# Double output tiles stored 256 tokens at a time, with the orders and engines drawn anew, in a fused sparse attention and max-out kernel

## The chip, the cores and the metric

The kernel runs on one NeuronCore of a Trainium2 chip. The metric is the device time of one execution in microseconds (us). Each core has five engines that run side by side and meet through semaphores: TensorE (PE in the profile, with its weight loads as PEld), VectorE (DVE), ScalarE (ACT), GpSimd (POOL) and SyncE (SP), which here only issues transfers (DMAs).

## The reference

Inputs are q, k, v of shape (4 batches, 8 heads, 768 positions, 64) and three weights: w1 and w2 (512 x 1024) and w_out (1024 x 512), all float32.

```
k_sum = k.reshape(B, H, nb, 32, D).max(axis=3)       # one key per block of 32
v_sum = v.reshape(B, H, nb, 32, D).mean(axis=3)
scores_l = scale * q @ k^T, kept where |i - j| < 16
scores_s = scale * q @ k_sum^T + log(32)
a = softmax over [scores_l, scores_s]
x = a @ [v, v_sum]                                    # heads side by side: 3072 tokens x 512
out = maximum(x @ w1, x @ w2) @ w_out                 # 3072 x 512, float32
```

## The kernel before, in words

Work is cut by batch (b, 0 to 3), by pair of heads (hp, 0 to 3) and by group of 256 tokens (grp, 0 to 2, NG = 3). For every batch and pair, k, q and v are loaded (`load_kq` L450, `load_v` L461) into one of 13 landing tiles, cast to bf16 (`prep` L572, `cast_v` L471), and k and q are turned so that the head dimension lies on partitions: by PE (L593), or, for the pairs in `turn` (batch 2, pairs 2 and 3, and batch 3), by a transposing DMA (L597). The turned k is placed, its block maxima are taken (L619), and tails and maxima are put beside it. `scores` (L661) fills two PSUM banks per group, `weigh` takes the exponential on ACT (L675) and the mask on DVE (L685), `values` multiplies by v on PE (L717), DVE divides (L738, L741), and the result xs is turned into xt, by PE in batch 0 and by a DMA on SP (L747) in batches 1 to 3.

`maxout` (L821) uses max(h1, h2) = h1 + max(h2 - h1, 0). Weights wd = w2 - w1 are made on the chip (L777), and w1o = w1 @ w_out (`make_w1o`, L805, matmuls L813), which needs w1 turned (L787) and w_out cast (L802). For each of the 12 groups there are four "hidden" tasks (L829, 8 matmuls each), each followed by a relu on ACT (L838) or DVE (L840) into g, and two output tiles of 128 tokens (u = 0, 1). An output tile is three tasks on PE in one PSUM bank: x @ w1o (L856, 4 matmuls) and two halves of g @ w_out (L863, 4 matmuls each). Then ACT or DVE copies the bank into an SBUF tile `o` (L866), and SP stores that tile of 128 x 512 float32 (256 KB) in one DMA (L874). Tokens are shifted by 16, so the last tile of a batch wraps and takes two DMAs (L874 and L876). The very last tile is cut in three parts (256, 128 and 128 columns).

Nothing of the order is in program order. Each step is a task of a `Plan` (L116), with a priority from `CFG["prios"]` and, where there is a choice, an engine from `CFG["engines"]`, one entry a task. `Plan.run` (L182) plays the tasks through with durations written in the program and writes each engine's instructions in the order that comes out; what a queue then waits for, the whole queue behind it waits for. Buffers come from rings (`Ring`, L69): a task may take a slot only when the planner believes the slot's last user to be done. `osr` (L332) is the ring of output tiles, 4 slots. At most eight of SP's DMAs are under way: each waits for the eighth before it. Matmuls with no use (`filler`, L300) stand where the planner expects PE to be idle early.

Of the kernel before, what the change touches and what calls it, by code (L numbers as in the profile page):

```python
# [14 lines left out]
F32 = mybir.dt.float32  # L15
# [12 lines left out]
    turn="22 23 30 31 32 33", lx="SSS", cols=True,  # L28
)
CFG["prios"] = list(map(int, """  # L30
# [25 lines left out]
""".split()))  # L56
CFG["engines"] = "".join("""
PDDDPPADDDPPPPPPDPSSSDDDATDASSSDDPPTAASSSPPDPTAASSSPDPPTDDSSDPTASSPDTASSPATDSSDATASPSPSASPDTDTADPDADDTATADPPADATATDD
PPAAATPTDDAAPDTATDDTDTATDDTATATDDTDTATDDTDTATDDTATATDDTASSSDSSSASSSASSSPPDDPDDDATDDDDDATATADPDAADTATDDPADATADTDDSTAD
TDDSTADTDDSPTDTDDPAPDDTPTADDDPDTADTDDSTADTDDSTADTDDSSSSDSSSASSSASSSADPADPAAATAAPAPATATDDAAPDDTATADPPDDTADTDDSTADTDDS  # L60
TADTDDSDSASADPAPASDSDDPADTADTDDSTADTDDSTADTDDSSSSASSSASSSPSSSDPAPADSPDTDPPDAPSDSDDADDPSDSADDAATADTDDSTADTDDSTADTDDSA
SPSDDPPAASDSDDADATADTDDSTADTDDSTADTDDSTTATTDTTATTATDTDTATATTTASTTTASTATATATDTTTASTTTDSTATATATATTTASTTTDSTDTATDTDTTTA
STTTASTDTATDTDTTTASTTTASTATDTDTDTTTASTTTASTDTATDTDTTTASTTTDSTATATATATTTDSTTTASTDTATATDTTTASTTTASTATATDTDTTTDSTTTDSTA
TATDTATTTDSTTTASTDTATATATTTDSTTTASTTTDATTTDS
""".split())
ENG = {"T": "PE", "D": "DVE", "A": "ACT", "P": "POOL", "S": "SP"}

# [192 lines left out]
def kernel(  # L260
# [14 lines left out]
    nc = tc.nc  # L275
# [53 lines left out]
    xsr = Ring(tiles("xs", 4, [128, 2, 2, 2, D], BF16))  # L329
    xtr = Ring(tiles("xt", 6, [128, KC, GT], BF16))  # L330
    gr = Ring(tiles("g", 3, [128, FC, GT], BF16))
    osr = Ring(tiles("o", 4, [128, d_model], F32))  # L332
    wd = [Buf(Ring([t])) for t in tiles("wd", 4, [128, KC, 256], BF16)]
    w1br = Ring(tiles("w1b", 2, [128, KC, 256], BF16))
    w1b = [Buf(w1br) for _ in range(4)]
# [485 lines left out]
    def maxout(b, grp, prio):  # L821
        x, g = xt[b, grp], Buf(gr)
        for n in range(4):
            ps = Buf(banks, "mm")

            def hid(n=n, ps=ps):
                for s in range(2):
                    for c in range(KC):
                        nc.tensor.matmul(out=bank(ps)[:, 256 * s:256 * s + 256],  # L829
                                         lhsT=wd[n].ap[:, c, 128 * s:128 * s + 128],  # L830
                                         rhs=x.ap[:, c, :], start=(c == 0), stop=(c == KC - 1))

            op("T", 0.87, lambda e, hid=hid: hid(), words=16, read=[x, wd[n]], write=[ps], prio=prio, label=f"hidden {b}{grp}{n}")

            def relu(e, n=n, ps=ps):
                o = g.ap[:, 2 * n:2 * n + 2, :].rearrange("p f n -> p (f n)")
                if e == "A":
                    nc.scalar.activation(out=o, in_=bank(ps), func=ACT.Relu)  # L838
                else:
                    nc.vector.tensor_scalar_max(out=o, in0=bank(ps), scalar1=0.0)  # L840

            op("A", {"A": 0.6, "D": 0.69}, relu, read=[ps], write=[g], prio=-1, label=f"relu {b}{grp}{n}")
        last = b == B - 1 and grp == NG - 1
        for u in (1, 0) if last else (0, 1):
            o = Buf(osr)
            cuts = (0, 256, 384, 512) if last and u == 0 else (0, 512)
            for i, (c0, c1) in enumerate(zip(cuts, cuts[1:])):
                out_part(b, grp, u, x, g, o, c0, c1, prio, "D" if i == 1 else "A", i == 1)

    def out_part(b, grp, u, x, g, o, c0, c1, prio, engine, on_act):  # L850
        ps, cols, part = Buf(banks, "mm"), slice(c0, c1), (c1 - c0) / 512
        sl, done = slice(128 * u, 128 * u + 128), Buf(Ring([None]))

        def first():
            for c in range(KC):
                nc.tensor.matmul(out=bank(ps, c1 - c0), lhsT=x.ap[:, c, sl], rhs=w1o[c].ap[:, cols],  # L856
                                 start=(c == 0), stop=False)

        op("T", 0.87 * part, lambda e: first(), words=8, read=[x, *w1o], write=[ps], prio=prio + 1, label=f"out {b}{grp}{u}")
        for n in range(2):  # L860
            def more(n=n):
                for f in range(4 * n, 4 * n + 4):
                    nc.tensor.matmul(out=bank(ps, c1 - c0), lhsT=g.ap[:, f, sl],  # L863
                                     rhs=wo[f // 2].ap[:, f % 2, cols], start=False, stop=(f == FC - 1))
            op("T", 0.87 * part, lambda e, more=more: more(), words=8, read=[g, *wo], change=[ps], prio=prio + 1, label=f"out {b}{grp}{u}")
        copy(engine, {"A": 0.18 + 0.42 * part, "D": 0.15 + 0.55 * part}, lambda: (  # L866
            o.ap[:, cols], bank(ps, c1 - c0)),
             read=[ps], write=[o, done], prio=-1, port=False, label=f"copy out {b}{grp}{u}")

        def store(e):  # L870
            at = grp * GT + u * 128 + 16
            n = min(128, S - at)
            queue = nc.scalar if on_act else nc.sync
            queue.dma_start(out=out[b * S + at:b * S + at + n, cols], in_=o.ap[0:n, cols])  # L874
            if n < 128:
                queue.dma_start(out=out[b * S:b * S + 128 - n, cols], in_=o.ap[n:128, cols])  # L876

        op("A" if on_act else "S", 0.75 * part, store, read=[done], touch=[o], prio=-1, issue=0.65, label=f"store {b}{grp}{u}")

    def attention(b, base):  # L880
        for half in range(2):
# [78 lines left out]
```

## Time and profile before

| | us |
|---|---|
| median of 3 runs (lowest, highest) | 170.51 (169.4, 171.54) |
| the profiled execution | 169.97 |
| its span, from first to last recorded instruction | 168.2 |
| PE busy in it | 159.7 |

The profiled execution lies 0.54 us below the median, and 1.77 us of it lie outside the span. A group row of the profile names a line, an engine, the operation, the output and input tiles, the count, the busy time, the mean duration in ns, and the idle time before it with what ended it. The chain of waits is read from the end back: each piece is what released the next one. A DMA on SP has two times: how long SP was held by it (SPq), and how long after its issue the data had landed. The granted TensorE clock was 1.00 in every stage.

### The profile page before, as it was taken

How to read it: one execution, taken by the hardware profiler on the slowest of the kernel's cores; microseconds unless marked ns; L12 is line 12 of the kernel's file. 1: busy time of each engine (PE TensorE's matmuls, PEld its weight loads, DVE VectorE, ACT ScalarE, POOL GpSimd, SP SyncE). 2: the span in 40 equal slices, each digit the busy share in tenths (PEclk: the TensorE clock that was granted, in tenths of full speed). 3: DMA queues.
4: the chain of work that ended last, by engine and by line, in shares of the span. 5: the costliest groups of instructions: out<-in, count | busy, mean ns of one | idle time of the engine just before them, and what ended most of it. 6: DMA issues, size and time to landing. Idle time of an engine off the chain costs nothing.

```text
span 168.2 us, 4640 instructions
## 1 busy us (share of the span) xinstructions
PE 159.7 (95%) x1918; PEld 105.6 (63%) x1918; DVE 104.0 (62%) x207; ACT 104.5 (62%) x148; POOL 43.1 (26%) x73
## 2 busy tenths in 40 slices
PE   6999999989999999999999999979997999999992
PEld 4768757765676555667577555737564558568462
DVE  4778688663397898787695573849913867023031
ACT  4576888783697998887993578953365652024111
POOL 7506575056534000356330203330300000000000
PEclk9999999999999999999999999999999999999999
DMA  5999999999999999999888998989889336211033
GB/s 166 337 227 329 283 348 351 375 376 313 302 281 320 304 277 233 290 179 216 173 190 241 293 170 212 248 116 238 163 251 162 94 66 181 41 62 64 4 125 125
DMA packets 69829, 36.68 MB, mean 218 GB/s; under 512 B 54640, under 2 KB 65776, under 8 KB 69808
## 3 DMA queue, kind: packets, MB, share of 16 engines
q1 hardware_dynamic: 69664, 36.32, 86.1%
q8 instruction: 15, 0.25, 0.7%
q10 hardware_dynamic: 144, 0.07, 0.1%
q14 instruction: 6, 0.05, 0.1%
HBM read 25.17 MB, written 6.29 MB: 187 GB/s over the span
## 4 chain that ended last, share of the span: by engine, by line
PE 70%; DMA 14%; SPq 9%; POOL 3%; issue 1%; DVE 0%; ACT 0%
PE banks L863 24%; PE banks L829 20%; PE banks L856 11%; DMA land<-in_moe_w_out_dram 6%; DMA land<-in_v_dram 4%; PE banks L813 4%; SPq L463 4%; PE banks L717 4%; PE banks L661 3%; DMA kt<-kqb 3%; SPq L454 3%; PE banks L593 2%; DMA xt<-xs 1%; SPq L597 1%; PE banks L537 1%; POOL vx L565 1%
## 5 line engine op out<-in xcount | busy, mean ns | idle before, releaser
L829 PE MATMUL banks<-xt,wd 128*128 128x256 bf16 x384 | 46.2, 273 | 1.5 <-DMA xt<-xs 1.2
L863 PE MATMUL banks<-wo,g 128*128 128x512 bf16 (+2 forms) x208 | 46.8, 363 | 0.0
L829 PEld LDWEIGHTS <-wd 128*128 128x128 bf16 x384 | 37.2, 98 | 10.3 <-issue 1.5
L863 PEld LDWEIGHTS <-g 128*128 128x128 bf16 x208 | 19.0, 98 | 17.1
L675 ACT ACTIVATE pb<-banks 128x1024 bf16<-128x1024 f32 x24 | 23.8, 1021 | 8.1 <-PE banks L661 8.0
L838 ACT ACTIVATE g<-banks 128x512 bf16<-128x512 f32 x27 | 16.0, 596 | 20.1 <-PE banks L829 19.9
L856 PE MATMUL banks<-w1o,xt 128*128 128x512 bf16 (+2 forms) x104 | 24.6, 363 | 0.0
L840 DVE TENSOR_SCALAR g<-banks 128x512 bf16<-128x512 f32 x21 | 14.3, 687 | 10.1 <-PE banks L829 10.0
L619 DVE TENSOR_REDUCE ks<-kx 128x24 bf16<-128x768 bf16 x16 | 15.1, 949 | 5.7 <-ACT kx L565 5.3
L565 ACT COPY o<-banks 128x512 f32<-128x512 f32 (+1 forms) x16 | 9.1, 575 | 15.3 <-PE banks L863 13.2
L685 DVE TENSOR_TENSOR pb<-pb,mask 128x1024 bf16<-128x1024 bf16 (+1 forms) x24 | 12.6, 557 | 7.8 <-ACT pb L675 7.7
L565 ACT CAST kqb<-land 128x768 bf16<-128x768 f32 x14 | 13.9, 995 | 3.9 <-DMA land<-in_q_dram 1.9
L741 DVE TENSOR_TENSOR xs<-banks,inv 128x512 bf16<-128x512 f32 x24 | 15.9, 678 | 0.3
L565 DVE COPY o<-banks 128x512 f32<-128x512 f32 (+1 forms) x10 | 6.0, 608 | 13.9 <-PE banks L863 13.9
L856 PEld LDWEIGHTS <-xt 128*128 128x128 bf16 x104 | 9.3, 98 | 8.3 <-DMA xt<-xs 0.2
L565 POOL COPY vx<-vx 32x128 bf16<-32x128 bf16 (+5 forms) x10 | 7.6, 769 | 21.7 <-DVE vx L491 12.5
L303 PE MATMUL banks<-ident,identity 128*128 128x256 bf16 x70 | 10.9, 308 | 1.6 <-DVE identity L354 1.6
L661 PEld LDWEIGHTS <-kx 64*128 64x128 bf16 x416 | 7.0, 94 | 7.5 <-issue 7.4
L717 PEld LDWEIGHTS <-pb 128*64 128x64 bf16 (+1 forms) x384 | 8.9, 110 | 4.0 <-issue 1.9
L717 PE MATMUL banks<-vx,pb 128*64 128x65 bf16 (+1 forms) x384 | 11.0, 196 | 0.0
L593 PE MATMUL banks<-ident,kqb 128*128 128x128 f32 x60 | 10.0, 282 | 0.3 <-ACT kqb L565 0.2
L565 DVE CAST kqb<-land 128x768 bf16<-128x768 f32 x12 | 8.2, 693 | 3.3 <-DMA kt<-kqb 1.9
(84 smaller groups left out, 183.9 us busy)
## 6 DMA issues: line engine op xcount, KB each, us to landing
land<-in_k_dram SPq DMA_DIRECT2D x16, 384.0 KB, 6.2
land<-in_q_dram SPq DMA_DIRECT2D x16, 384.0 KB, 5.9
land<-in_v_dram SPq DMA_DIRECT2D x16, 384.0 KB, 6.3
out_dram<-o SPq DMA_DIRECT2D x19, 256.0 KB, 3.9
land<-in_moe_w_dram SPq DMA_DIRECT2D x8, 512.0 KB, 8.2
land<-in_moe_w_out_dram SPq DMA_DIRECT2D x4, 512.0 KB, 9.7
out_dram<-o SPq DMA_DIRECT2D x4, 224.0 KB, 4.3
xt<-xs SPq DMA_TRANSPOSE x18, 2.6
```

Source lines behind the costliest of these rows:

```text
L565: {"D": nc.vector.tensor_copy, "A": nc.scalar.copy, "P": nc.gpsimd.tensor_copy}[e](out=o, in_=i)
L593: nc.tensor.transpose(out=bank(ps)[:, 128 * j:128 * j + 128], in_=src.ap[:].bitcast(F32)[:, 128 * j:128 * j + 128], identity=ident32[:])
L619: op("D", 0.95, lambda e: nc.vector.tensor_reduce(out=ks.ap[:, 0:nb], in_=free(kt(), 128, [256, NM], [192, 2], [32, 2], [1, 32]), axis=AX. ...
L675: op("A", {"A": 1.03}, lambda e: nc.scalar.activation(out=spread(pb.ap[:, 0, 0:1], [192, 8], [128, 2], [1, 64]) if PW > 128 else spread(pb ...
L685: nc.vector.tensor_tensor(out=o, in0=o, in1=spread(mask[:, 2 * u:2 * u + 1, 0:1], [0, n], [64, 2], [1, 64]), op=ALU.mult)
L717: nc.tensor.matmul(out=o, lhsT=p[r], rhs=vx[b].ap[r, par, hp + n, 2 * grp + u, a, 0:D + 1], start=(PW == 128 or par == 0), stop=(last and ...
L741: op("D", 0.69, lambda e: nc.vector.tensor_tensor(out=x.ap[:].rearrange("p n u a d -> p n (u a) d"), in0=spread(bank_tile[:, ps.ap, 0:1], ...
L829: nc.tensor.matmul(out=bank(ps)[:, 256 * s:256 * s + 256], lhsT=wd[n].ap[:, c, 128 * s:128 * s + 128], rhs=x.ap[:, c, :], start=(c == 0), ...
L838: nc.scalar.activation(out=o, in_=bank(ps), func=ACT.Relu)
L840: nc.vector.tensor_scalar_max(out=o, in0=bank(ps), scalar1=0.0)
L856: nc.tensor.matmul(out=bank(ps, c1 - c0), lhsT=x.ap[:, c, sl], rhs=w1o[c].ap[:, cols], start=(c == 0), stop=False)
L863: nc.tensor.matmul(out=bank(ps, c1 - c0), lhsT=g.ap[:, f, sl], rhs=wo[f // 2].ap[:, f % 2, cols], start=False, stop=(f == FC - 1))
```

## The change

Output tiles of groups 0 and 1 of a batch lie in one double tile [128, 2, 512], and one DMA of 256 tokens (512 KB) stores both halves when both have been copied. Group 2, whose second half wraps around, is stored in single tiles as before, out of the two halves of a double tile. `osr` has two double slots in place of four single ones, so the SBUF is the same. A group takes its slot before its first copy and keeps it until its last store has landed.

```diff
-    osr = Ring(tiles("o", 4, [128, d_model], F32))
+    osr = Ring(tiles("o", 2, [128, 2, d_model], F32))
...
+        o = Buf(osr)
         for u in (1, 0) if last else (0, 1):
-            o = Buf(osr)
...
-            o.ap[:, cols], bank(ps, c1 - c0)),
+            o.ap[:, u, cols], bank(ps, c1 - c0)),
...
+            if whole:
+                queue.dma_start(out=out[at - 128:at + 128].rearrange("(u p) c -> p u c", u=2), in_=o.ap)
+                return
+            queue.dma_start(out=out[at:at + n, cols], in_=o.ap[0:n, u, cols])
...
+        whole = grp < NG - 1
+        if whole and u == 0:
+            return
+        op("A" if on_act else "S", 1.45 if whole else 0.75 * part, store, read=[o if whole else done], touch=[o], prio=-1,
+           issue=0.65, words=16 if whole else 8, label=f"store {b}{grp}{u}")
```

Both tables, `prios` and `engines`, are replaced, so every engine's list has a new order. What that moves, counted in the lists of both kernels:

- SP has 115 entries for 122: 8 stores of 256 tokens and 13 smaller ones in place of 29, and one more copy of v's rows by DMA (L563).
- PE has the same real matmuls, and 68 fillers for 70. In front of the first w1o task stand two more hidden tasks (L829 on group 1 of batch 0) and one more turn of k (L593). Among the tasks from there to the end PE goes over 49 times for 42 between short matmuls (scores, values, sums) and long ones.
- In the early loads, two weight loads stand ahead of the load of q of batch 1, and two k loads of batch 1 stand between the first and the second of the four w_out loads (one k load stood ahead of all four).
- Of the four subtractions wd POOL makes one and DVE three (two and two before). The first three w1b casts stand on POOL, POOL and ACT, the last on DVE.
- All six DMAs xt of batch 2 stand ahead of the turn of k for pair 0 of batch 3; before, two of them stood behind it. The last turn (q of batch 3) has two stores of 256 tokens in front of it; before, three of 128.
- DVE has 22 entries more in its list, ACT 8 and POOL 15 fewer.

More of the change, by code (lines that the diff above doesn't have):

```diff
@@ L30 @@
 CFG["prios"] = list(map(int, """
[25 rows of a table removed]
[25 rows of a table added]
 """.split()))
 CFG["engines"] = "".join("""
[L58 to L64, printed above, removed]
+PDDDPDADPAPPDDDDDPSSSDADATADSSSDPDPTADSSSPAPATADSSSDDPPTAASSDPTASSPPTDSSDATASSDDTDSASPSDSPDTPTADAPPAATPTDDAADDDTDTDD
+AAPAATPTDDPAADTATDDTDTATDDTDTATDDTATATDDTDTATDDTATATDDTDSSSDSSSASSSASSSPDDDDDDDPTDDDDDDTATADDPDDDTATDDADPDTADTDDSTAD
+TDDSTADTDDSDTDTDDAAPADTDTADADADTADTDDSTADTDDSTADTDDSSSSDSSSASSSASSSAPPAPPAAPTAAPPPATATDDDADDDTATADDPDDTADTDDSTADTDDS
+TADTDDSDSASADDDAASDSADPDDTADTDDSTADTDDSTADTDDSSSSASSSDSSSDSSSDDSDPPSPATAAPPDPSDSDDDDDDSDSDDDDPTADTDDSTADTDDSTADTDDSA
+SASADDPPDSASADDPATADTDDSTADTDDSTADTDDSTTDTTATTDTTDTATATATATTTATTTASTDTATATATTTATTTDSTDTATATATTTASTTTDSTDTDTDTDTTTDTT
+TDSTDTATATDTTTATTTASTDTATDTATTTASTTTDSTATATATDTTTATTTDSTATDTATDTTTATTTASTDTDTDTDTTTDSTTTASTATATATATTTATTTASTATATATDT
+TTATTTDSTATDTDTATTTASTTTASTTTDATTTDS
 """.split())
@@ L866, in out_part @@
         copy(engine, {"A": 0.18 + 0.42 * part, "D": 0.15 + 0.55 * part}, lambda: (
-            o.ap[:, cols], bank(ps, c1 - c0)),
+            o.ap[:, u, cols], bank(ps, c1 - c0)),
              read=[ps], write=[o, done], prio=-1, port=False, label=f"copy out {b}{grp}{u}")
         def store(e):
[L871 to L874, printed above, removed]
-            if n < 128:
-                queue.dma_start(out=out[b * S:b * S + 128 - n, cols], in_=o.ap[n:128, cols])
-        op("A" if on_act else "S", 0.75 * part, store, read=[done], touch=[o], prio=-1, issue=0.65, label=f"store {b}{grp}{u}")
+            queue, at = nc.scalar if on_act else nc.sync, b * S + grp * GT + u * 128 + 16
+            n = min(128, (b + 1) * S - at)
+            if whole:
+                queue.dma_start(out=out[at - 128:at + 128].rearrange("(u p) c -> p u c", u=2), in_=o.ap)
+                return
+            queue.dma_start(out=out[at:at + n, cols], in_=o.ap[0:n, u, cols])
+            if n < 128:
+                queue.dma_start(out=out[b * S:b * S + 128 - n, cols], in_=o.ap[n:128, u, cols])
+        whole = grp < NG - 1
[3 more added lines that the diff above has]
+           issue=0.65, words=16 if whole else 8, label=f"store {b}{grp}{u}")
     def attention(b, base):
```

50 rows, old and new, of the table turn are left out of this document.

## The prediction

> **What bounds the kernel.** I read the page first, then PE's waits, the busy time by stage, and the chain of waits with the timelines around its breaks.
>
> ```profile
> span 168.2 us, 4640 instructions
> PE 159.7 (95%) x1918; PEld 105.6 (63%) x1918; DVE 104.0 (62%) x207; ACT 104.5 (62%) x148; POOL 43.1 (26%) x73
> ```
>
> PE is busy for 95% of the span, the others for at most 63%. All of PE's idle time that a wait explains is in seven rows, of which these matter:
>
> ```profile
> PE banks L829 <- DMA xt<-xs: 1.2, 1, 1.2
> PE banks L661 <- DMA kt<-kqb: 1.0, 1, 1.0
> PE banks L813 <- POOL wo L565: 0.8, 1, 0.8
> PE banks L787 <- POOL w1b L565: 0.4, 1, 0.4
> PE banks L829 <- DVE wd L777: 0.2, 1, 0.2
> ```
>
> Three lie early and two late. The stages 37.30 to 90, to 111 and to 165 us sum to
>
> ```profile
> sum 127.70, PE 125.51; mean PE 41.84
> ```
>
> so from the first w1o matmul on PE stands still for only 2.19 us, the first two rows. Before it PE waits for loads, and fillers cover that. The chain of waits (start, duration, what) gives the price of PE's tasks and the breaks:
>
> ```profile
> 37.30 2.75 PE banks L813 x12
> 40.05 0.87 PE banks L829 x8
> ...
> 44.39 0.33 PE banks L593 x3
> ...
> 62.31 0.86 PE banks L856 x4
> 63.17 0.38 PE banks L717 x16
> 63.55 0.97 PE banks L863 x4
> ...
> 108.58 2.32 SPq L597
> ...
> 111.00 2.49 DMA xt<-xs
> ...
> 124.01 5.13 DMA kt<-kqb
> ...
> 164.99 0.02 issue
> ```
>
> A hidden task costs 0.87 us, a turn 0.33, four output matmuls 0.86, but 0.97 behind a short task: a change from short to long matmuls costs 0.11. Each late break comes from SP: an xt issued at 111.00 behind a turn that held SP for 2.32 us, and a turn that took 5.13 us to land.
>
> So the time is the start of w1o (37.30), PE's work from there (125.51), the gaps (2.19), and 3.2 from PE's last matmul (164.99) to the end. Times that I give "by the list" are estimates: PE's new order played from its new start with these prices, and what hangs on it with the durations of its rows.
>
> **The change, step by step.**
>
> *Fewer stores.* 29 store issues on SP become 21, the same bytes. No row of PE names a store, so this alone gains nothing; its value is room on SP before the turns.
>
> *Start of w1o.* Ahead of it PE now does two hidden tasks and one turn more: 2 x 0.87 + 0.33 = +2.07 us. The three early waits (0.75 + 0.40 + 0.25 = 1.40) get other causes:
>
> ```profile
> 24.27 0.62 PE L787 MATMUL banks<-identity,w1b 128*128 128x128 bf16 x8 [0.40 <-POOL w1b L565]
> 32.44 1.05 PE L829 MATMUL banks<-xt,wd 128*128 128x256 bf16 x8 [0.25 <-DVE wd L777]
> 31.16 1.22 DVE L777 TENSOR_TENSOR wd<-land,land 128x1024 bf16<-128x1024 f32 x1 [1.35 <-DMA land<-in_moe_w_dram]
> 34.94 1.04 POOL L565 CAST wo<-land 128x1024 bf16<-128x1024 f32 x1 [6.69 <-DMA land<-in_moe_w_out_dram]
> 36.21 1.04 POOL L565 CAST wo<-land 128x1024 bf16<-128x1024 f32 x1 [0.23 <-DMA land<-in_moe_w_out_dram]
> ```
>
> Loads of 512 KB land 36.21 - 34.94 = 1.27 us apart. The wd for the last early hidden task of group 0 needed the sixth weight load, landed at 31.16; now it needs the seventh, so about 32.4, and is ready 1.22 later, at 33.7. PE would be there at 32.44 - 0.65 + 1.15 (a w1 turn, 0.6 by the first row, and a values task of batch 0, taken as 0.55, come ahead) = 32.9: a wait of 0.8. Behind that subtraction DVE has this work in turn before PE can go on to group 1:
>
> ```profile
> L741 DVE TENSOR_TENSOR xs<-banks,inv 128x512 bf16<-128x512 f32 x24 | 15.9, 678 | 0.3
> ...
> L840 DVE TENSOR_SCALAR g<-banks 128x512 bf16<-128x512 f32 x21 | 14.3, 687 | 10.1 <-PE banks L829 10.0
> ...
> L565 DVE CAST kqb<-land 128x768 bf16<-128x768 f32 x12 | 8.2, 693 | 3.3 <-DMA kt<-kqb 1.9 <-DMA land<-in_q_dram 1.1 <-issue 0.3
> ...
> L738 DVE RECIPROCAL inv<-banks 128x8 f32<-128x8 f32 x24 | 4.8, 203 | 8.4 <-PE banks L717 6.4 <-PE banks L722 1.8
> ...
> L565 DVE CAST w1b<-land 128x1024 bf16<-128x1024 f32 x1 | 0.8, 800 | 0.6 <-DMA land<-in_moe_w_dram 0.6
> ```
>
> relu, reciprocal (0.2), xs, cast and w1b: 0.69 + 0.2 + 0.68 + 0.6 (the shorter of the casts) + 0.8 = 3.0, to 36.7; PE arrives there at 33.7 + 2 x 0.87 + 0.6 = 36.1: another 0.6. So 1.4 goes and 1.4 comes. The w_out load that the first w1o task needs has one more k load ahead of it: about 36.21 + 1.0 + 1.05 for its cast on ACT = 38.3, before PE arrives, so that wait is gone. w1o starts at 37.30 + 2.07 = 39.4. Bounds: no early wait 38.3 (the load), both twice as long 40.8. I take 39.4, since each wait is a difference of rows.
>
> *PE's work behind it.* -2.07, and 49 changes between short and long matmuls for 42: 7 x 0.11 = +0.77. Sum -1.30.
>
> *The late gaps.* The xt that came late stood behind a turn on SP. Now all six xt of batch 2 stand ahead of those turns. By the list, the last values task of batch 2 that a group needs ends 9.7 us of PE work before that group; before it was 6.6, and 7.8 was needed. The 1.2 goes. What is late next: group 0 of batch 1 now follows its values task by 5.65 us (9.4 before), and the first group of batch 3 by 4.9. Needed: 0.2 + 0.68 on DVE and the landing,
>
> ```profile
> out_dram<-o SPq DMA_DIRECT2D x19, 256.0 KB, 3.9
> land<-in_q_dram SPq DMA_DIRECT2D x16, 384.0 KB, 5.9
> land<-in_moe_w_dram SPq DMA_DIRECT2D x8, 512.0 KB, 8.2
> xt<-xs SPq DMA_TRANSPOSE x18, 2.6
> kt<-kqb SPq DMA_TRANSPOSE x12, 2.8
> ```
>
> 2.6: 3.5 together, so 2.1 and 1.4 are left for SP's queue. I take no wait; bound 0 to 1.2 each (the one seen).
>
> The turn that came late stood behind three stores (landing 5.13 for a median of 2.8). Its cast now stands on DVE behind a relu that ends at about 121.1 and a maximum; 122.9 by the list, landing 125.7 at the median, and PE needs it at about 128.0. The 1.0 goes; bound: it stays. So -2.19 in all.
>
> *Double tiles.* A slot is kept from a group's first copy until the store of both halves has landed. The closest hand-over is from group 1 of batch 1 to group 2: copied at about 93.1, the next copy at 99.2, so 6.1 us. The store's price is unknown: 3.9 (256 KB store) to 8.2 (512 KB load). I take 6, between them, since half the bytes are a store's; at 8.2 ACT waits 2.1 us in a place where its next work (the sums of batch 3) comes at 103. The uncopied tiles hold PSUM banks, and PE, which needs one again at 103.8, stops if the store takes over 10 us. Cost 0, up to 2 at the bound. The Trainium skill ("DMA: Bandwidth & Descriptors", Anatomy of one DMA) puts a transfer at about 2.0 us plus its bytes at 436 GB/s, and by that a store of 512 KB takes 3.2 us, an estimate from that page. The rows of this case, 3.9 and 8.2, lie above it; by the page the hand-over has 2.9 us to spare, and the sum is the same.
>
> *Tail.* The tile that is copied last but one now wraps, one DMA more ahead of the last 128 columns:
>
> ```profile
> 162.40 0.42 SPq L876 DMA_DIRECT2D out_dram<-o  x1
> 163.43 2.23 SPq L874 DMA_DIRECT2D out_dram<-o  x3
> ```
>
> 0.42 for it, of which the last three's spacing hides a little: +0.3.
>
> Sum: 2.07 - 1.30 - 2.19 + 0.3 = -1.1 us, on a span of 168.2: 167.1, and 168.9 for the profiled execution. That one lies 0.5 below the median, so 169.4 us for the median.
>
> **Rivals.**
> 1. The gain is given back: new waits at the two xt, or the early loads at their later bound. 1.2 + 1.4 more: 172.0. For it: the margins of 1.4 and 2.1 us, less than one turn's hold on SP (2.32 in the chain). Against: SP has eight issues fewer.
> 2. Slower: batch 3's last q loads come late on SP. They now stand behind two more turns and one more xt (1.2 us each by the second row below) and three store issues fewer:
>
> ```profile
> 95.35 3.83 SPq L597 DMA_TRANSPOSE kt<-kqb  x1
> ...
> 107.31 1.23 SPq L747 DMA_TRANSPOSE xt<-xs  x1
> ```
> ```profile
> L565 ACT COPY kx<-kt 128x768 bf16<-128x768 bf16 x2 | 3.1, 1530 | 0.7 <-DMA kt<-kqb 0.7
> ```
>
> By the list the load of q for pair 2 is issued at about 110 and lands at 116; ACT casts it, then places two k at 1.53 each, DVE takes the maxima, and the scores wait with 1.3 us to spare. From 1.3 us late, PE loses one for one. A double store in the wrong place (SP waits for both halves, and all loads behind it) can make SP 6 us late: 169.4 + 4.7 = 174.1, over 2% slower from 5.3 us late. Against: the longest that one DMA held SP between the first store and the tail was 3.83 us.
> 3. The last turn lands behind the double stores, 1 MB, issued 3.5 us ahead of it. At 8.2 us they land at 127.7; if the turn waits for them and then needs its 2.8, PE stops for 2.4: 171.8. For it: 5.13 behind three stores. The Trainium skill ("DMA: Bandwidth & Descriptors", Queues, rings and completion order) says that a DMA's count lands only after every earlier write of the same engine, which is this mechanism; by that rule the 5.13 in the chain agrees.
> 4. Faster: the early waits are not there (38.3, -1.1) and the tail hides: 168.0; over 2% needs 167.1, so 0.9 more that I don't see.
>
> **How the numbers follow.** Forecast 0.5; rivals 1 and 3 together 0.24, rival 2 0.18, rival 4 0.08. 2% (3.4 us) is about what a measurement of this kernel can tell from no change: its runs lie 2.1 us apart. Faster over 2% 0.07 (most of it rival 4 with more gone), slower 0.17 (rival 2), within 0.76. The range: rival 4 with the runs' spread below (168.0 - 1.0) gives 167.0; rival 1's 172.0 with 1.0 of spread gives 173.0. The likeliest's own range is 168.0 to 171.0.
>
> **What would show it.** PE's first w1o row near 39.4; no wait of L829 for xt nor of L661 for kt; 115 SP issues with 8 stores of 512 KB; ACT's or DVE's copies of o waiting at most 2 us for out_dram; PE's last matmul near 163.6. Wrong: a PE wait over 1 us behind 40, or w1o after 41.

## The result, and the profile after

| | before | after |
|---|---|---|
| median (lowest, highest), us, 20 runs each on one chip | 169.44 (167.99, 171.54) | 170.63 (169.5, 172.94) |
| span of the profiled execution, us | 168.2 | 169.8 |
| first w1o matmul, us | 37.30 | 38.00 |
| last matmul's end, us | 165.21 | 166.52 |

The ratio is 1.0095, with a 95% interval of 1.007 to 1.012: slower by 1.2 us, where 1.1 us of gain were forecast. Ratios, here and below, are of undisturbed runs; medians are of all runs, so the two need not agree to the last digit. Each group of experiments ran on one chip with runs of the kernel before between them.

The page and PE's waits after the change:

```profile
span 169.8 us, 4594 instructions
PE 157.8 (93%) x1896; PEld 105.2 (62%) x1916; DVE 110.2 (65%) x229; ACT 98.5 (58%) x140; POOL 38.1 (22%) x58
```
```profile
PE banks L829 <- DMA xt<-xs: 1.7, 1, 1.7
PE banks L829 <- ACT o L565: 0.7, 1, 0.7
PE banks L537 <- ACT vx L565: 0.7, 1, 0.7
PE banks L661 <- DMA kt<-kqb: 0.7, 1, 0.7
```

PE shows 1896 matmuls where 1916 weight loads stand: some 20 matmul records are missing, so PE's busy sums of the two traces are not compared here; waits and starts are. The two waits behind the start of w1o that were to go (2.19 us) have become four, 3.77 us. Where they lie (start, duration, the wait in brackets), first after, then before, with the rows at which w1o starts, PE ends and, at 113.22, a group begins that matters later:

```profile
38.00 2.32 PE L813 MATMUL banks<-wo,w1t 128*128 128x512 bf16 x9
...
70.99 0.84 PE L537 MATMUL banks<-vx,amean 128*32 128x256 bf16 x24 [0.70 <-ACT vx L565]
83.49 1.91 PE L829 MATMUL banks<-xt,wd 128*128 128x256 bf16 x16 [1.67 <-DMA xt<-xs]
95.75 1.03 PE L829 MATMUL banks<-xt,wd 128*128 128x256 bf16 x8 [0.72 <-ACT o L565]
...
113.22 1.04 PE L829 MATMUL banks<-xt,wd 128*128 128x256 bf16 x8
131.47 0.29 PE L661 MATMUL banks<-kt,kx 64*128 64x64 bf16 x8 [0.68 <-DMA kt<-kqb]
165.46 1.06 PE L863 MATMUL banks<-wo,g 128*128 128x128 bf16 x16
```
```profile
113.53 1.91 PE L829 MATMUL banks<-xt,wd 128*128 128x256 bf16 x16 [1.21 <-DMA xt<-xs]
129.28 0.41 PE L661 MATMUL banks<-kt,kx 64*128 64x64 bf16 x16 [0.98 <-DMA kt<-kqb]
164.15 1.06 PE L863 MATMUL banks<-wo,g 128*128 128x128 bf16 x16
```

Between the first w1o matmul and the last matmul's end lie 127.91 us before and 128.52 after. Less the waits, PE's work is 125.7 before and 124.75 after, about 1.0 less. So the 1.6 us between the spans are: start +0.70, work -1.0, waits 3.77 - 2.19 = +1.6, and the tail behind the last matmul 2.99 to 3.28, +0.3.

The wait at 83 us is that of the group that the prediction named as next in line, group 0 of batch 1. SP and DVE there:

```profile
76.60 0.69 DVE L741 TENSOR_TENSOR xs<-banks,inv 128x512 bf16<-128x512 f32 x1
77.16 1.23 SPq L747 DMA_TRANSPOSE xt<-xs  x1
78.49 1.76 SPq L597 DMA_TRANSPOSE kt<-kqb  x1
80.34 1.22 SPq L747 DMA_TRANSPOSE xt<-xs  x1
```

Its xs was ready at 77.29, but SP issued another group's xt and a turn first; the xt was issued 3.05 us later and took 3.1 more to land. The wait at 95.75 is for a home (a free double tile): ACT could not copy until the double store issued at 87.91 had landed, 7.13 us later, and PE lacked a bank.

```profile
95.12 1.07 ACT L565 COPY o<-banks 128x512 f32<-128x512 f32 x2 [1.89 <-DMA out_dram<-o]
```

One more view matters later: the share of the DMA engines (last but one column: the time that their packets took, of the time of 16 engines) and the GB/s that they moved (last column), here in three stretches, first before, then after.

```profile
60.00:88.00 28.00, 28.00 (x351) 17.32 (x350) 23.33 (x47) 24.59 (x32) 9.61 (x13) 1.00 1.03 221
88.00:113.00 25.00, 24.32 (x311) 15.05 (x310) 14.17 (x32) 16.89 (x22) 5.14 (x5) 1.00 1.00 217
113.00:130.00 17.00, 15.49 (x161) 10.04 (x160) 10.51 (x18) 7.52 (x14) 1.76 (x4) 1.00 0.98 202
```
```profile
60.00:88.00 28.00, 25.11 (x298) 15.49 (x301) 20.83 (x44) 21.61 (x26) 9.87 (x12) 1.00 1.06 198
88.00:113.00 25.00, 23.93 (x309) 15.18 (x313) 19.81 (x40) 11.18 (x17) 4.34 (x4) 1.00 1.01 228
113.00:130.00 17.00, 16.84 (x140) 10.78 (x142) 11.12 (x21) 9.54 (x10) 1.77 (x3) 1.00 0.95 209
```

Up to 130 us the engines look full in either kernel, and the prediction read only PE's column of such rows. But a share near 1.00 does not show that there was no room: here it passes 1.00 (1.03 and 1.06), and at such shares the engines moved 198 to 228 GB/s, where the page of the changed kernel has 351 to 380 GB/s between 21 and 38 us. Slice by slice (40 slices of 4.2 us, busy tenths, 9 is 90% or more) that page also has gaps, 6 tenths from 110.4 to 114.6 us among them:

```profile
DMA  5999999999999998999969998969996146330034
```

So a transfer that lands late is not explained by these shares alone.

### The profile page after: what moved, and what is told of

It is laid out like the page before. It is cut to its first block, busy times and chain, and to the rows that moved or that the text cites. A ratio compares the mean times of both kernels' runs of the same rounds, so it can differ in the third digit from the quotient of the medians.

```text
span 169.8 us, 4594 instructions
## 1 busy us (share of the span) xinstructions
PE 157.8 (93%) x1896; PEld 105.2 (62%) x1916; DVE 110.2 (65%) x229; ACT 98.5 (58%) x140; POOL 38.1 (22%) x58
## 4 chain that ended last, share of the span: by engine, by line
DMA 33%; PE 33%; SPq 12%; ACT 8%; DVE 6%; issue 4%; POOL 1%; DVEq 0%; ACTq 0%; POOLq 0%
PE banks L863 12%; PE banks L829 11%; DMA land<-in_q_dram 9%; DMA land<-in_moe_w_out_dram 6%; PE banks L856 6%; DMA land<-in_moe_w_dram 5%; SPq L454 5%; DMA land<-in_v_dram 4%; DMA out_dram<-o 4%; DMA kt<-kqb 4%; SPq L597 3%; ACT pb L675 3%; SPq L463 3%; PE banks L717 2%; DVE ks L619 2%
## 5 line engine op out<-in xcount | busy, mean ns | idle before, releaser
L829 PE MATMUL banks<-xt,wd 128*128 128x256 bf16 x384 | 46.6, 273 | 2.4 <-DMA xt<-xs 1.7
L863 PE MATMUL banks<-wo,g 128*128 128x512 bf16 (+2 forms) x195 | 44.5, 362 | 1.0 <-issue 0.6
L829 PEld LDWEIGHTS <-wd 128*128 128x128 bf16 x384 | 36.9, 98 | 10.1 <-issue 2.9
L863 PEld LDWEIGHTS <-g 128*128 128x128 bf16 x208 | 18.7, 98 | 16.9
L856 PE MATMUL banks<-w1o,xt 128*128 128x512 bf16 (+2 forms) x98 | 23.9, 362 | 0.3
L840 DVE TENSOR_SCALAR g<-banks 128x512 bf16<-128x512 f32 x20 | 13.8, 688 | 15.9 <-PE banks L829 15.8
L838 ACT ACTIVATE g<-banks 128x512 bf16<-128x512 f32 x28 | 16.7, 599 | 12.1 <-PE banks L829 12.0
L565 ACT CAST kqb<-land 128x768 bf16<-128x768 f32 x12 | 11.6, 967 | 10.1 <-DMA kt<-kqb 5.5
L565 POOL COPY vx<-vx 32x264 bf16<-32x264 bf16 (+5 forms) x11 | 7.7, 702 | 35.0 <-ACT vx L565 29.0
L685 DVE TENSOR_TENSOR pb<-pb,mask 128x512 bf16<-128x512 bf16 (+1 forms) x24 | 12.4, 551 | 3.0 <-ACT pb L675 2.9
L565 DVE CAST kqb<-land 128x768 bf16<-128x768 f32 x16 | 10.5, 656 | 2.3 <-DMA land<-in_q_dram 1.2
L565 ACT CAST vx<-land 128x768 bf16<-128x768 f32 x6 | 5.1, 842 | 11.8 <-DMA land<-in_v_dram 11.8
L303 PE MATMUL banks<-ident,identity 128*128 128x256 bf16 x68 | 9.9, 301 | 1.8 <-DVE identity L354 1.8
```

The costliest lines, as they stand in the source:

```text
L303: nc.tensor.matmul(out=bank_tile[:, slot, 0:256], lhsT=identity[:], rhs=ident32[:].bitcast(BF16), start=True, stop=True)
L565: {"D": nc.vector.tensor_copy, "A": nc.scalar.copy, "P": nc.gpsimd.tensor_copy}[e](out=o, in_=i)
L685: nc.vector.tensor_tensor(out=o, in0=o, in1=spread(mask[:, 2 * u:2 * u + 1, 0:1], [0, n], [64, 2], [1, 64]), op=ALU.mult)
L829: nc.tensor.matmul(out=bank(ps)[:, 256 * s:256 * s + 256], lhsT=wd[n].ap[:, c, 128 * s:128 * s + 128], rhs=x.ap[:, c, :], start=(c == 0), ...
```

## The experiments

In all of them every engine's list stays as the planner of the one or the other kernel wrote it; edits are made behind the planning, so what differs is what the diff shows. `move` takes one entry of the finished list to another place (written here in one form for all):

```
+def move(order, label, at, behind=0):
+    t = next(t for t in order if t.label == label)
+    order.remove(t)
+    order.insert(next(i for i, o in enumerate(order) if o.label == at) + behind, t)
```

Theory A says that the double tiles cost the time, theory B that the new order does.

**e1_four_homes: four double tiles, the order held.**

```
-    osr = Ring(tiles("o", 2, [128, 2, d_model], F32))
+    homes = tiles("o", 4, [128, 2, d_model], F32)
+    osr = plan.osr = Ring(homes[0:2])
...
+        turn = {b: None for t in order for b in t.new if b.ring is self.osr}
+        for n, b in enumerate(turn):
+            b.slot = n % len(self.homes)
```

> The changed kernel with every list of every engine kept as it is, and four double tiles of output in place of two, taken in turn. Theory A (the double tiles themselves cost the time: a home is kept until 512 KB have landed): ACT's and DVE's waits for out_dram ahead of the copies of o (6.7 us in 3) go, PE's wait of 0.7 us in L829 for a copy of o goes, and the time falls by 0.7: 169.9, ratio to the kernel before 1.005. Theory B (the new order costs it: an xt behind a turn on SP, a late vx, a turn behind stores): the waits of 1.7, 0.7 and 0.7 stay, and what PE gains of the 0.7 is given back at the next of them: 170.6, ratio 1.007 to 1.010.

Ratio 1.0088 (1.0053 to 1.0123). The waits for a home are gone from ACT, DVE and PE; xt waits of 0.4 and 0.9 and a kt wait of 0.9 stand. The ratio is B's, though the waits are not those that B expected to stay: the home was a wait, but taking it away gained nothing.

**e2_single_stores and e11_order_alone: the halves stored singly.** Each half goes by its own DMA as soon as it is copied; e11 has four homes as well, so nothing is left but the order.

```
-            if whole:
-                queue.dma_start(out=out[at - 128:at + 128].rearrange("(u p) c -> p u c", u=2), in_=o.ap)
-                return
```

> The changed kernel with its lists held, but each 128-token half is stored by a DMA of its own as soon as it is copied (8 issues more on SP; the homes are the same two double tiles). Theory A: the first half of a home comes free earlier and no 512 KB stand in front of a turn, so the 0.7 us of PE for a copy of o shrinks to 0.3 or less and the 0.7 for kt goes: 169.5 to 169.9, ratio 1.000 to 1.003. Theory B: the xt wait of 1.7 and the vx wait of 0.7 stay, and with 8 more issues on SP (0.65 each) the xt comes no earlier: 170.6, ratio 1.007 or above.

> The changed kernel's lists held, without what the doubles cost: every half stored by its own DMA as soon as it is copied, and four double homes, so that no copy waits for a home. What is left is the new order. If the order alone costs the time: as e2_single_stores, ratio 1.005 to 1.009, with xt waits of 1 us or more near 83 or 113 and w1o starting near 38.5. If doubles and homes together are the cost: 1.000 to 1.003.

e2 1.0069 (1.0037 to 1.0101), e11 1.013 (1.0099 to 1.0161). Without what the doubles cost the new order is no faster than with it (two of e11's six executions had a granted clock of 0.988 and 0.989; they took 171.87 and 171.19 us, the other four 171.22 to 171.70). In e11 the only wait of PE over 0.2 us behind the start of w1o is the xt of batch 1's group 0, and it has grown:

```profile
83.67 3.23 PE L842 MATMUL banks<-xt,wd 128*128 128x256 bf16 x16 [2.50 <-DMA xt<-xs]
```

**e3_before_double, e7_before_double_tail, e9_before_late_halves: the double stores in the old order.** Three homes, because the old order has three groups open at a time. In e7 the last group but one is stored in halves at their own places; in e9 every double store is two DMAs at its place.

```
+                if plan.home[b, grp, "halves"] == 2:
+                    at += b * S - u * 128
+                    nc.sync.dma_start(out=out[at:at + 256].rearrange("(u p) c -> p u c", u=2), in_=home[:])
```
```
-            if grp < NG - 1:
+            if grp < NG - 1 and (b, grp) != (3, 1):
```
```
-                    nc.sync.dma_start(out=out[at:at + 256].rearrange("(u p) c -> p u c", u=2), in_=home[:])
+                    for half in range(2):
+                        nc.sync.dma_start(out=out[at + 128 * half:at + 128 * half + 128], in_=home[:, half])
```

> The kernel before, with all its lists held, but with double tiles and one DMA of 512 KB in place of the later of the two stores of a group. Three homes, since its order has three groups open at a time and two homes would not do. Theory A: slower than before by what the doubles cost, about 0.7 to 1.4: 170.1 to 170.8, ratio 1.004 to 1.008. Theory B: the doubles cost nothing where homes are enough, and there are four store issues fewer in front of the late turn of 0.98: 169.4 or up to 0.5 less, ratio 0.997 to 1.000.

> The kernel before with its lists held, and double tiles and stores as in e3_before_double, except that group 1 of batch 3, whose store is the last but one, is stored in two halves as before. Theory T (what the doubles cost in the old order is the tail, 3.4 us against 3.0, since 512 KB are issued just ahead of the last 64 KB): the tail is 3.0 again, 0.4 less than in e3_before_double, ratio 1.004 to 1.006. Theory Q (512 KB at a time on the queue make loads, xt and turns land later all along): ratio stays at 1.008. If e3_before_double's figure was mostly its spread: 1.000 to 1.003.

> The kernel before with its lists held and double tiles as in e3_before_double, but each double store is two DMAs of 256 KB at the place of the later one. Theory L (the doubles cost time in the old order because the first half leaves only when the second is copied, so that more is under way when the next transposing DMAs come, and those hold SP: the first xt held it 4.17 us in e3_before_double and 1.37 before): the same as e3_before_double, ratio 1.008. Theory Z (it is the size, one DMA of 512 KB that lands later than two of 256 KB): as the kernel before, 1.000 to 1.003.

e3 1.0081 (1.0041 to 1.012), e7 1.0132 (1.0079 to 1.0185), e9 1.0067 (1.0027 to 1.0108). So in the old order the doubles do cost 0.7 to 1.3%, and theory B alone does not hold there. It is not the tail: e7's is 3.0 again and it is no faster, above both of its forecasts. It is not the size either: e9 moves 256 KB at a time and is as slow, within the intervals. What the three share is that the first half leaves late. SP, before and in e3 (the first two xt):

```profile
68.53 3.41 SPq L747 DMA_TRANSPOSE xt<-xs  x2
```
```profile
67.19 5.48 SPq L760 DMA_TRANSPOSE xt<-xs  x2
```

The two xt hold SP 2.1 us longer; in e9 it is 0.4. Counted from each one's w1o start, the xt that PE waited for at 113.5 before is issued at 73.7 before, 74.8 in e3 and 75.7 in e7, but at 73.8 in e9. That the late half is what fills the queue is argued from e3 and e7, and e9 does not show it; the profiled executions of e3 and e9 were the shortest of their runs and show no loss.

**e4_xt_first and e6_homes_xt: the late xt ahead of the turn, with two homes and with four.**

```
+        move(order, "xt 100", "turn k23")
```

> The changed kernel with one move on SP: the last xt of group 0 of batch 1 is issued ahead of the turn of k for pair 3 of batch 2, not behind it. Theory B: it was issued at 80.3 behind a turn that was held until 80.25; ahead of it it is issued at about 78.5 and lands 1.8 earlier, so PE's wait of 1.7 in L829 goes, and the time falls by up to 1.7: 168.9, ratio 0.997. If the turn, 1.3 us later then, is itself in need (the copies of kx on ACT wait for kt at 82.8), PE waits in L661 for up to 1.3 instead: 170.2, ratio 1.005. Theory A: the time lies in the copies of o; PE reaches the wait of 0.7 for them 1.7 earlier and waits there 1.7 longer: 170.6, ratio 1.007.

> The changed kernel with both edits at once: four double homes, and the last xt of batch 1's group 0 ahead of the turn of k. Theory C (two limits in series: taking away the xt wait alone moved 1.7 us into the wait for o, which rose from 0.7 to 2.5, and taking away the o wait alone left the xt waits): with both away 1.7 + 0.7 = 2.4 us go, less what an xt of batch 2 or the last turn takes back (0.9 to 1.2 seen): 1.2 to 2.4 below the changed kernel, ratio 0.996 to 1.003. Theory D (neither is the cause, the new order's later start of w1o and the loads are): no gain, ratio 1.007 to 1.010.

e4 1.0124 (1.008 to 1.0168), e6 1.01 (1.0042 to 1.0157), both against what they were to gain. In e4 the xt wait is gone and the wait for a home has taken its time, 2.46 for 0.72:

```profile
96.65 1.03 PE L836 MATMUL banks<-xt,wd 128*128 128x256 bf16 x8 [2.46 <-ACT o L572]
```

In e6, with homes enough, xt waits of 1.58 and 1.21 stand near 83 and 113 (in an execution of 172.72 us; e6's shortest took 169.41). The xt was issued 1.55 us sooner (78.79 for 80.34 in the changed kernel) and landed 0.3 sooner (83.15 for 83.45): ahead of it a load of v and a store landed only at 81.50 and 82.32. In e4, where these two landed at 78.74 and 81.08, the same move brought the xt in at 81.92. So an earlier issue is worth what the transfers ahead of it leave of it.

The expectation of e6 had named another cause, theory D, the later start of w1o and the loads. Its ratio fits e6 too, and no run here moves that start.

**e5_after_again: the changed kernel once more.**

> The changed kernel once more, unedited, as the reference on the same chip. All theories: ratio 1.0095 to the kernel before, within 1.006 to 1.013. The trace shows which waits come back: an xt wait in front of group 0 of batch 1 near 83 us (1 us or more) and a wait for a copy of o near 95 (0.5 to 2.5, more where the xt wait is short) if theory C is right that two late arrivals stand in series there; the vx wait of 0.7 only if it is no accident of one execution.

1.0081 (1.0031 to 1.0131). The xt wait at 83 (1.09), the wait for a home at 96 (0.96) and the kt wait (1.00) came back, an xt wait of 0.34 stood at 113.74, and the vx wait did not come: 3.39 in all (in an execution of 172.72 us, where the median is 171.42). An early wait of 1.00 for wd stood where the prediction had put 0.8, and w1o started at 39.41.

**e8_homes_xt_turn and e12_stores_behind: the last turn and the stores.** e8 is e6 with one edit more; in it the turn stands ahead of its own cast, so one pair's q is not used there and the time is a lower bound at most; e12 does it properly.

```
+        move(order, "turn q31", "store 201")
```
```
+        move(order, "store 101", "turn q31", 1)
+        move(order, "store 201", "turn q31", 1)
```

> As e6_homes_xt, and the last turn (q of batch 3) is issued ahead of the two double stores in front of it. If those 1 MB make it land late (6.0 us for a median of 2.8), PE's wait of 0.4 to 0.9 in L661 goes, and the time is 0.5 to 0.9 below e6_homes_xt: ratio 0.992 to 0.998. If the turn is late because its cast ends late on DVE (125.4), the stores wait for it in vain, the turn is issued at the same time and lands at most 1 to 2 us sooner, and the wait shrinks only as far as the landing does; if the landing does not depend on the stores ahead, the ratio is that of e6_homes_xt.

> The changed kernel with one edit on SP: the two double stores of batches 1 and 2 stand behind the last turn (q of batch 3), not ahead of it. In e8_homes_xt_turn the turn was issued ahead of its cast, so that it turned what lay in the tile before and did not wait; here it waits for its cast. Rival 3 of the prediction (the last turn lands behind 1 MB of stores): its landing falls from 6.0 us towards the median of 2.8 to 3.8, PE's wait of 0.7 to 1.0 in L661 goes, ratio 1.003 to 1.006. If the cast on DVE, which ended at 125.4, is what makes it late: the landing shrinks, but the wait stays over 0.4 and the ratio at 1.007 to 1.010.

e8 1.0121 (1.0067 to 1.0174), e12 1.0088 (1.0052 to 1.0123), neither with the gain that rival 3 would have given. In e12 the turn landed in 4.2 us for 6.0 and the kt wait is gone: rival 3's mechanism is real. A copy of o now waits for the later store at nearly the same place, and PE with it:

```profile
130.58 1.02 PE L864 MATMUL banks<-w1o,xt 128*128 128x512 bf16 x4 [0.61 <-DVE o L573]
```

**e10_before_two_moves: the prediction's gain, done alone in the old order.**

```
+        move(order, "xt 202", "turn k30")
+        move(order, "turn q30", "store 200")
```

> The kernel before with two moves on SP, and nothing else: the xt that came late (group 2 of batch 2) is issued ahead of the turn of k that held SP for 2.3 us, and the turn that came late (q of batch 3) ahead of the three stores in front of it. This is the prediction's late-gaps step done alone. If that step was right in itself, 1.2 and 1.0 us go: 2.2 less, ratio 0.987. If the lateness is SP's and only passes to the next in line (the turn of k is 1.2 us later, the stores 1.5), a part of it comes back as other waits: ratio 0.995 to 1.000.

0.9978 (0.9935 to 1.0021), not 0.987. In its profiled execution (171.41 us, where its median is 170.42) the xt wait fell from 1.21 to 0.38 and 0.35 and the kt wait went, but other waits came in their place:

```profile
117.38 1.03 PE L837 MATMUL banks<-xt,wd 128*128 128x256 bf16 x8 [1.06 <-DVE g L848]
...
130.16 0.41 PE L669 MATMUL banks<-kt,kx 64*128 64x64 bf16 x16 [1.49 <-ACT pb L683]
```

**e13 to e16: a gate.** By now waits moved and the time did not. One candidate for what holds it is a start, called the gate here: the second group of batch 2 begins at 113.53 before, 113.71 in e9, 114.28 in e3, and 113.22, 113.74, 113.94, 113.42 in the changed kernel, e5, e2 and e6, when its last xt lands (of the runs so far the earliest is e1, 111.53, the latest e7, 115.92). From there to the last matmul's end, less later waits, PE works 165.21 - 113.53 - 0.98 = 50.7 us before and 166.52 - 113.22 - 0.68 = 52.6 after: the trace has two tasks more of output tiles there (116 weight loads of L863 for 108, four to a task of 0.87 us). The other executions agree: 50.6 to 50.9 with the old lists, 52.4 to 53.1 with the new (54.2 in e14, at a mean clock of 0.990).

Two things speak against the gate as the whole answer. In the changed kernel itself, in e4, e11 and e12 PE does not wait there. And the executions differ already in the start of w1o; counted from it, the gate's xt lands at 76.2 us before, and at 75.1, 75.4, 74.6, 74.3 and 73.1 us in the changed kernel, e2, e6, e5 and e1, so it does move. e13 issues the xt that group 0 of batch 1 waits for ahead of the other xt and the turn, with four homes; e14 adds e12's edit; e15 and e16 add to e13 and e14 that two stores get out of the gate's way.

```
+        move(order, "xt 100", "turn k23")
+        move(order, "xt 102", "xt 100", 1)
```
```
+        move(order, "store 121", "xt 222", 1)
+        move(order, "store 120", "xt 222", 1)
```

> The changed kernel with four double homes and, on SP, the xt of batch 1's group 0 that PE waits for at about 83 us issued ahead of the xt of group 2 and of the turn, so as soon as its xs is there (about 77.3, landing by 80.5). Theory D (what the new order lacks is the distance between the last values task of this group and the group): PE's xt wait near 83 is at most 0.3, no wait for o at 95; if nothing else takes it back, the time falls by 1.2: ratio 1.000 to 1.003. Theory P (what is made early at one place is late at the next, since SP's transposing DMAs come one behind the other): the xt waits near 87 or 113 or the kt wait near 131 grow by what was gained: ratio 1.007 to 1.012.

> As e13_xt_ahead_two, and the two double stores of batches 1 and 2 stand behind the last turn, not ahead of it. With four homes no copy has to wait for the later stores, as one did in e12_stores_behind (0.61 for DVE's copy of o). Theory D: no wait of PE over 0.4 is left behind 40 us but the xt near 113; start 38.5, work 124.6, tail 3.3 and 0.5 to 1.5 of waits make a span of 167.0 to 168.0, ratio 0.995 to 1.000. Theory P: other waits take their place, and the ratio stays at 1.005 or above.

> As e13_xt_ahead_two (four homes, the xt of batch 1's group 0 first), and on SP the stores of the last tiles of batch 1 stand behind the last two xt of batch 2, not among them. Theory G (a gate: whatever PE gains before, the second group of batch 2 starts when its last xt has landed, at 113.1 to 114.6 in the changed kernel and in its variants, and 52.7 us of PE work stand behind that in the new order against 50.7 in the old): its last xt is issued at about 108.3 in place of 110.6 to 111.4 and lands by 112.0, PE's wait of 2.07 near 114 falls under 0.8, and the time falls by 1.3 to 2.0 against e13_xt_ahead_two: ratio 1.004 to 1.008. Theory P (any move on SP only passes the lateness on): PE's waits behind 115 grow by as much (the turns, kt near 131), ratio 1.012 to 1.016.

> As e15_gate_first, and the two double stores of batches 1 and 2 stand behind the last turn as in e14_xt_and_stores. Theory G: neither an xt near 114 nor kt near 131 stops PE for more than 0.8; start 38.5, work 124.6, waits 1.0, tail 3.3: span 167.4, ratio 0.995 to 1.001. Theory P: 1.010 or above, with new waits behind 115.

e13 1.0164 (1.0109 to 1.0219), e14 1.012 (1.0041 to 1.0199): e13 is slower than either of its theories said. The waits at 83 and 95 are gone, and about as much is waited for at the gate (e13's row; e14's is 1.95, at a mean granted clock of 0.990):

```profile
114.57 1.05 PE L843 MATMUL banks<-xt,wd 128*128 128x256 bf16 x8 [2.07 <-DMA xt<-xs]
```

e15 1.0037 (0.9993 to 1.0081), e16 1.0071 (1.0035 to 1.0107), which lies between its two forecasts. SP in the changed kernel, where the xt of 110.59 is the gate's, and in e15:

```profile
105.57 0.58 SPq L454 DMA_DIRECT2D land<-in_q_dram  x1
106.25 0.67 SPq L876 DMA_DIRECT2D out_dram<-o  x1
107.01 1.21 SPq L747 DMA_TRANSPOSE xt<-xs  x1
108.32 1.71 SPq L876 DMA_DIRECT2D out_dram<-o  x1
110.08 0.42 SPq L878 DMA_DIRECT2D out_dram<-o  x1
110.59 2.50 SPq L747 DMA_TRANSPOSE xt<-xs  x2
```
```profile
104.34 0.58 SPq L470 DMA_DIRECT2D land<-in_q_dram  x1
105.02 5.12 SPq L763 DMA_TRANSPOSE xt<-xs  x3
110.24 1.00 SPq L892 DMA_DIRECT2D out_dram<-o  x2
```

With three stores taken out of its way the gate opens without a wait, at 110.44; 1.07 of that is lost again behind:

```profile
110.44 1.04 PE L845 MATMUL banks<-xt,wd 128*128 128x256 bf16 x8
...
122.40 1.02 PE L872 MATMUL banks<-w1o,xt 128*128 128x512 bf16 x4 [1.07 <-DVE g L856]
```

Moving nothing but stores at the gate is worth 1.3% against e13 (0.4% by the medians of all runs, 172.72 on 170.51 and 172.11 on 170.59) and 0.5% against e14 (1.1% by the medians). Only the first of these differences is clear of the intervals, and each pair was run on two chips, each run against the kernel before on its own. In the profiled executions w1o started at 39.81 in e13 and at 38.28 in e15, which no store at the gate can have moved; from there to the last matmul's end it is 127.77 and 126.58 us, 1.2 of the 2.7 us between the spans. So theory G holds in kind for these variants; how much of the changed kernel's time it explains is not shown. No version here is faster than the kernel before beyond its interval.

## Why the prediction was wrong, step by step

- *Fewer stores*: right that it gains nothing by itself. That its value is room on SP is not borne out: in the old order the double stores cost 0.7 to 1.3%.
- *Start of w1o*, +2.07: measured +0.70 in the profiled execution. The two tasks and the turn came. Early waits were 1.27 us, near the 1.4. Most of the rest is fillers, whose time fell by 1.0; I had not counted it. But 38.00 is the earliest of 13 executions with these early lists: the others lie at 38.2 to 39.8, the median of all is 38.46. Five with the old lists lie at 36.7 to 37.7, median 37.30. So the start is later by about 1.2 us, as much as the whole loss by the medians; it was in the forecast, with 2.07.

```profile
L303 PE MATMUL banks<-ident,identity 128*128 128x256 bf16 x70 | 10.9, 308 | 1.6 <-DVE identity L354 1.6
```
```profile
L303 PE MATMUL banks<-ident,identity 128*128 128x256 bf16 x68 | 9.9, 301 | 1.8 <-DVE identity L354 1.8
```

- *PE's work behind it*, -1.30: measured about -1.0. Right.
- *The late gaps*, -2.19: this is the step that failed. 3.77 us of waits stand in their place (3.39 in e5). "Needed: 0.2 + 0.68 on DVE and the landing" left out the queue: from xs to issue it was 3.05 us, and the landing 3.1, so about 7 us were needed where the list gave 5.65. I had seen this distance as next in line, had put its margin at 2.1, and took zero. My own figure for batch 2, 7.8 needed with the queue in it, stood in the same paragraph and would have given a wait of about 2.1; the measured one is 1.67. The other three waits (a home, vx, kt) come on top. Behind it lies a second mistake: I summed PE's waits as if each could be taken away. e1, e4, e6 and e13 took away waits of the new order and were no faster than it; e10 did my two gains alone and got 0.2%, within its interval. What keeps the time up when these waits go is open: the gate, with 1.9 us more of PE's work behind it, fits e13 against e15, but the later start of w1o is as large as the loss, and no run moved it.
- *The turn behind the stores*: I had it landing at 125.7. Its cast ended at 125.37, not 122.9, and behind two double stores it took 6.04 us to land. Rival 3 is the mechanism, at 0.7 us where I had priced 2.4; e12 shows that taking it away passes the wait to a copy of o.
- *Double tiles*, 0: the hand-over that cost PE 0.72 was from group 1 of batch 0 to group 1 of batch 1, not the one I called closest. The store took 7.13 us there, between the rows that I had as bounds; the median was 3.7 (8 stores). By the fit that the Trainium skill ("DMA: Bandwidth & Descriptors", Anatomy of one DMA) gives for transfers that GpSimd issues, it takes 3.2, an estimate; these stores go out from SP, and 3.2 is near their median but less than half of the one that mattered. e1, without this wait, is no faster.
- *Tail*, +0.3: measured +0.3.
- *Rivals*: rival 1, the gain given back by new xt waits, is what happened in part: one of its two xt waits came, the other did not, and a home, vx and kt made up the rest. Its 172.0 stood on a median of 170.51, and 1.0095 of that is 172.1; as the parts differ, that is partly luck. Rival 2 did not occur: no PE wait names the q loads. (Its "5.3 us late" for 2% should be 5.8, since 2% over 170.51 is 173.9.) Rival 4's early start of w1o (38.3) came in the profiled execution, its gain did not.
- *The range*: the measured median, 170.63, lies inside 167.0 to 173.0, but only because that range reaches as far as rival 1 and the kernel before came out at 169.44, 1.1 below the median that I started from; the change went the other way than forecast.

## What to carry to other kernels

Before waits are added up as gains, look for the next transfer that the engine would then wait for, and count the work behind it: a wait taken away ahead of it may only come back there (in e13, 2.07 us). The distance that a value needs between its maker and its user is the maker's work, its turn in the issuing queue and its landing behind all that is under way; medians of landings hide the last two. An edit that delays half of a buffer's transfer to save an issue may delay what the queue carries behind it (2.1 us in e3, 0.4 in e9).

## What the runs showed of the hardware

- A transposing DMA holds SP for 1.2 us when little is under way, and far longer in some places: 3.45 us for the turn at 95.88 in the changed kernel, behind two loads of v that took 7.3 and 8.5 us to land, and up to 5.0 us in e11. Plain loads are held too: one of v at 92.69, 3.09 us. What SP waits for inside, no run here shows.
- In 18 profiled executions, with 112 to 121 DMAs of SP each, no landing on record came ahead of that of a DMA issued earlier: the xt issued at 107.01 landed at 111.67, behind a store of 106.25 that landed at 111.19, though another xt needed 2.5 us. The Trainium skill ("DMA: Bandwidth & Descriptors", Queues, rings and completion order) says that a DMA's count lands only after the earlier writes of the same DMA engine; the trace agrees. It also says that completion is not first in, first out for an issuing engine, which no run here shows.
- Stores of 512 KB landed in 3.7 us in the median, loads of 512 KB (w1, w2) in 8.6. One DMA of 512 KB or two of 256 KB at the same place made no measurable difference (e3, e9).
- The same instructions gave 169.5 to 172.94 us in 20 runs; the start of w1o alone moved by 1.4 us between two executions of the changed kernel (38.00, 39.41).
